# K and Q turned by VectorE in SBUF, chunk bounds and selection by pairs of pairs, fewer multiplied masks, and a new order of work

## The chip, the cores and the metric

The kernel runs on one core of a Trainium2 chip. The core has five engines with an instruction stream each: TensorE (PE; its weight loads are listed apart as PEld), VectorE (DVE), ScalarE (ACT), GpSimd (POOL) and SyncE (SP), which here issues nearly all DMAs. Sixteen DMA engines move the data. The metric is the device time of one execution in microseconds (us).

## The reference

Two layers follow one another. The first is attention on selected chunks: for each query the keys are cut into 24 chunks of 32, an upper bound of the score with any key of a chunk is worked out from the chunk's smallest and largest key, the six best chunks that are not in the future are kept, and softmax runs over them alone. The second is a feed-forward layer with a hard swish.

```python
# q, k, v: (4, 8, 768, 64) fp32; chunk = 32, top_k = 6, scale = 1/8
k_min, k_max = min and max of k over each chunk
ub = sum over d of max(q * k_min, q * k_max)            # (4, 8, 768, 24)
ub = where(query's chunk >= chunk, ub, -1e9)
top_chunks = argsort(ub)[..., -6:]
scores = scale * q @ k.T
scores = where(chunk selected & causal, scores, -1e9)
attn = exp(scores - max) / (sum + 1e-9)
x = (attn @ v) as (3072, 512)
h = x @ w_in                                            # w_in (512, 2048)
out = (h * clip(h + 3, 0, 6) / 6) @ w_out               # w_out (2048, 512)
```

## The kernel before

The 32 heads are worked as 16 pairs, numbered 0 to 15; a pair's two heads e = 0, 1 lie in partitions 0 to 63 and 64 to 127, so that both of a pair's K (or Q) fill 128 partitions with the head dimension along them and the 768 positions along the free axis. Queries below 192 (Q0) see at most six chunks, so nothing is selected for them; the selection is for the other 576.

The whole program is one list of steps, `ORDER` (lines 34 to 111), written out by hand or by a planner that is not part of the file. The loop at line 619 emits the steps in this order, and each engine and the SP queue run what falls to them in it. Semaphores hold an instruction until its inputs are there and its output buffer is free; the order itself is never changed at run time. A late input therefore holds up everything behind it on that engine. A step is named by a short word and its indices, for example `S.7.3.a`: the scores of pair 7, unit 3, into the PSUM buffer a. PSUM holds three large buffers a, b and c (1,024 columns of fp32) and two small ones x and y (512).

For pair i the steps are:

- `lk.i`, `lq.i`, `lv.i`: loads of K, Q and V from DRAM by SP. For K and Q (line 215) there is one DMA for each head, with rows of 64 fp32, 256 bytes, as runs; three buffers each take turns. V is one DMA.
- `K.i`, `Q.i`: six 128x128 fp32 transposes by TensorE (line 298) into a large PSUM buffer, for the load lays positions along the partitions.
- `kb.i`, `qb.i`: ScalarE writes bf16 copies (lines 319 and 329). `mx.i`, `mn.i`: VectorE reduces the chunks of K (line 344). `rp.i`: ScalarE writes the positive part of Q; `rn.i` (VectorE) or `ra.i` (ScalarE) the negative part.
- `U.i`: the bounds, as (positive part of q) times k_max plus (negative part of q) times -k_min, fp32 matmuls into 96 partitions (line 367), and `ub.i`: VectorE adds the causal bias. Or `ud.i`, line 391: the same for the pairs i and i + 1 at once, in 128 partitions, with `us.i` for the bias. Before, pairs 0 to 5 go alone and pairs 6 to 15 in doubles.
- `T.i`: the bounds are transposed by TensorE (lines 403, 408), so that a query's 24 chunks lie along the free axis; `t8.i`: twelve instructions that give the eight largest of 32 (line 413); `sel.i`: each bound against the sixth largest (line 417); `L.i`: TensorE transposes the selection back (line 427); `mt.i`: VectorE copies it to SBUF.
- The mask is used in one of two ways. Pairs with an `sm` step (here 6 to 15) are multiplied: `sm.i` stores the selection to DRAM by four DMAs, `ml.i.j` loads it spread over the 32 keys of each chunk, for key block j, by six DMAs, `am.i.j` (GpSimd) cuts the causal corner, and `mu.i.u` (VectorE, line 463) multiplies the exponentials by it. The other pairs (0 to 5) add a large number to the scores by further matmuls (line 479).
- `S.i.u`: scores of unit u, one of six groups of key and query blocks (line 471); `ex.i.u`: exponentials by ScalarE (line 485); `af.i.u`: causal corner by GpSimd; `A.i`, `B.i.e`: the values (line 508), `na.i`, `nb.i`: normalised by VectorE into the input of the next layer.

The second layer runs over eight groups g of 384 tokens: `xt.g` turns the input by three DMA transposes (groups 0 and 1: `X` by TensorE); `H.g.f` is a pair of 128-wide slices of the hidden layer, eight matmuls (line 552); `hu` (ScalarE) and `gt` (VectorE, line 563) apply the gate; `O.g.t.n` is a quarter of the projection of 128 tokens (line 590), `ot` copies it out on ScalarE and `st` stores it. `wl.n` loads an eighth of the weights in fp32 (0 to 3 of w_in, 4 to 7 of w_out), in two buffers, and `wc.n` casts it to bf16 on GpSimd. These buffers later hold masks.

Of the kernel before, what the change touches and what calls it, by code (L numbers as in the profile page):

```python
# [15 lines left out]
P = 128  # L16
# [3 lines left out]
E_VAL = 8192.0  # L20
# [14 lines left out]
PRD Z.b.12 PRP PRL PRA lk.0 K.0.a lq.0 kb.0 mx.0 mn.0 Q.0.b rp.0 qb.0 lk.1 K.1.c rn.0 U.0.a ub.0 kb.1 mx.1 lq.1  # L35
Q.1.b T.0.x mn.1 t8.0 sel.0 lq.2 Q.2.a lk.2 lv.0 lq.3 lk.3 lv.1 rp.1 qb.1 ra.1 U.1.c ub.1 lk.4 vc.0 lv.2 lq.4
rp.2 qb.2 ra.2 K.2.b kb.2 L.0.y mt.0 S.0.1.c ex.0.1 S.0.2.a T.1.x S.0.3.c ex.0.2 ex.0.3 S.0.5.a ex.0.5 mx.2 mn.2
S.0.0.b ex.0.0 t8.1 sel.1 U.2.c ub.2 S.0.4.a ex.0.4 L.1.y Q.3.b rp.3 mt.1 S.1.1.c ex.1.1 qb.3 T.2.x t8.2 rn.3
K.3.a kb.3 af.0.5 af.0.3 af.0.0 af.0.1 A.0.y S.1.0.c ex.1.0 mx.3 sel.2 mn.3 S.1.4.b ex.1.4 S.1.2.c ex.1.2 L.2.x
S.1.5.b ex.1.5 vc.2 af.0.2 S.1.3.a ex.1.3 U.3.c mt.2 S.2.2.b ex.2.2 S.2.0.a ex.2.0 af.1.0 na.0 af.1.1 ub.3 T.3.x  # L40
t8.3 af.1.3 sel.3 af.2.2 af.1.5 K.4.c lq.5 kb.4 mx.4 S.2.3.b Q.4.a ex.2.3 B.0.0.y L.3.x mt.3 rp.4 lk.5 wl.0 lv.4
lq.7 S.2.1.b ex.2.1 vc.1 wc.0 af.2.0 af.1.2 af.2.1 B.0.1.y qb.4 mn.4 A.1.x S.3.1.b ex.3.1 S.3.2.c ex.3.2 S.2.5.b
ex.2.5 rn.4 U.4.a nb.0 S.3.0.c ex.3.0 na.1 ub.4 S.2.4.b ex.2.4 T.4.y t8.4 sel.4 K.5.a kb.5 mx.5 S.3.5.c ex.3.5
Q.5.b B.1.0.x L.4.y rp.5 mt.4 qb.5 B.1.1.x mn.5 S.4.2.c af.3.0 ex.4.2 rn.5 A.2.y lv.3 S.3.3.a ex.3.3 af.2.5 lk.7
lk.6 lq.8 lq.6 vc.3 wl.2 S.4.1.b U.5.c na.2 nb.1 ub.5 ex.4.1 vc.4 af.3.2 af.2.3 S.4.3.a ex.4.3 af.4.3 af.3.5
af.3.3 bd af.3.1 S.4.4.b ex.4.4 wc.2 af.4.1 af.4.2 T.5.y S.4.0.c S.3.4.a B.2.0.x S.4.5.b ex.4.0 ex.4.5 af.4.0
# [68 lines left out]
def kernel(  # L115
# [115 lines left out]
    def k_turn(i):  # L231
        nc.sync.dma_start_transpose(KB[i % 3][:], SK[i][:])
# [419 lines left out]
```

## Time and profile before

| | |
|---|---|
| median of three timed runs | 282.7 us (282.19 to 283.12) |
| profiled execution | span of 282.4 us, 0.3 us under that median |
| granted clock of TensorE | 1.00 throughout |
| busy: TensorE, VectorE, ScalarE, GpSimd | 271.8, 195.1, 182.1, 72.1 us |
| moved by DMA | 54.39 MB in 107,056 packets |
| of these under 512 B | 86,928 packets |

In the profile a busy time is the union of an engine's instructions. Matmuls are pipelined: one that stands at 379 ns follows the one before it by less, so the prices of TensorE's steps are taken from distances of starts. The page's slices cut the span into 40 equal parts of 7.06 us with the busy share in tenths. The chain of waits is the work that ended last, followed back to what released it. In a row of the groups stand line, engine, operation, output and input with their shapes, the count, the busy sum, the mean of one in ns, and the idle time before it. In a row of the DMA issues stand count, size, and the median time from issue to landing.

### The profile page before, as it was taken

How to read it: one execution, taken by the hardware profiler on the slowest of the kernel's cores; microseconds unless marked ns; L12 is line 12 of the kernel's file. 1: busy time of each engine (PE TensorE's matmuls, PEld its weight loads, DVE VectorE, ACT ScalarE, POOL GpSimd, SP SyncE). 2: the span in 40 equal slices, each digit the busy share in tenths (PEclk: the TensorE clock that was granted, in tenths of full speed). 3: DMA queues.
4: the chain of work that ended last, by engine and by line, in shares of the span. 5: the costliest groups of instructions: out<-in, count | busy, mean ns of one | idle time of the engine just before them, and what ended most of it. 6: DMA issues, size and time to landing. Idle time of an engine off the chain costs nothing.

```text
span 282.4 us, 6943 instructions
## 1 busy us (share of the span) xinstructions
PE 271.8 (96%) x2706; PEld 164.7 (58%) x2706; DVE 195.1 (69%) x523; ACT 182.1 (64%) x242; POOL 72.1 (26%) x138
## 2 busy tenths in 40 slices
PE   8798999899999999998999999999999999999995
PEld 3566777757654666564556566645456646555544
DVE  4787786979898896568975798737935894532330
ACT  2699999988758988452888865753657433433331
POOL 6034294486254031005531120107004100000000
PEclk9999999999999999999999999999999999999999
DMA  8999999979979998599999789998789320111023
GB/s 167 218 201 214 269 218 245 281 230 311 272 227 284 245 195 195 150 273 264 251 278 207 146 183 206 257 294 164 206 255 267 97 40 37 39 56 62 15 75 111
DMA packets 107056, 54.39 MB, mean 193 GB/s; under 512 B 86928, under 2 KB 96144, under 8 KB 107024
## 3 DMA queue, kind: packets, MB, share of 16 engines
q1 hardware_dynamic: 105456, 53.56, 77.8%
q10 hardware_dynamic: 1568, 0.39, 0.7%
q8 instruction: 21, 0.34, 0.6%
q14 instruction: 11, 0.09, 0.1%
HBM read 42.34 MB, written 9.24 MB: 183 GB/s over the span
## 4 chain that ended last, share of the span: by engine, by line
PE 73%; DMA 8%; ACT 5%; SPq 5%; DVE 4%; issue 2%; POOL 1%; ACTq 0%
PE PSy L590 13%; PE PSx L590 11%; PE PBb L552 10%; PE PBa L552 8%; PE PBc L552 8%; ACT PT L485 4%; DMA WS<-in_moe_w_in_dram 3%; PE PSx L508 3%; DMA QS<-in_q_dram 3%; DMA KSM<-in_k_dram 3%; PE PSy L508 2%; PE PBa L298 2%; PE PBc L471 2%; SPq L449 2%; PE PBb L290 2%; PE PBa L471 2%
## 5 line engine op out<-in xcount | busy, mean ns | idle before, releaser
L552 PEld LDWEIGHTS <-WIN 128*128 128x128 bf16 x512 | 48.9, 98 | 32.8 <-issue 1.3
L590 PEld LDWEIGHTS <-GT 128*128 128x128 bf16 x368 | 34.4, 98 | 37.9 <-issue 2.5
L590 PE MATMUL PSy<-WOUT,GT 128*128 128x512 bf16 x208 | 50.5, 379 | 0.0
L590 PE MATMUL PSx<-WOUT,GT 128*128 128x512 bf16 x160 | 38.9, 379 | 0.0
L552 PE MATMUL PBb<-XT,WIN 128*128 128x384 bf16 x192 | 35.1, 326 | 0.0
L485 ACT ACTIVATE PT<-PBc 128x1024 bf16<-128x1024 f32 (+2 forms) x34 | 31.4, 924 | 3.9 <-PE PBc L471 3.2
L485 ACT ACTIVATE PT<-PBb 128x1024 bf16<-128x1024 f32 (+2 forms) x35 | 31.3, 895 | 3.8 <-PE PBb L471 2.0
L456 POOL TENSOR_SCALAR_AFFINE_SELECT WS<-WS 128x256 bf16<-128x256 bf16 x30 | 12.5, 427 | 71.6 <-DMA WS<-SCR 51.8
L560 ACT ACTIVATE U<-PBb 128x768 bf16<-128x768 f32 x24 | 19.5, 811 | 16.3 <-PE PBb L552 16.3
L552 PE MATMUL PBa<-XT,WIN 128*128 128x384 bf16 x160 | 29.3, 326 | 0.0
L563 DVE SCALAR_TENSOR_TENSOR GT<-U,PBb 128x768 bf16<-128x768 bf16 x24 | 22.8, 950 | 9.4 <-ACT U L560 9.1
L552 PE MATMUL PBc<-XT,WIN 128*128 128x384 bf16 x160 | 29.3, 326 | 0.0
L508 PEld LDWEIGHTS <-PT 128*128 128x128 bf16 x672 | 24.8, 98 | 6.1 <-POOL PT L492 1.7
L463 DVE TENSOR_TENSOR PT<-PT,WS 128x256 bf16<-128x256 bf16 (+2 forms) x70 | 27.4, 441 | 0.0
L485 ACT ACTIVATE PT<-PBa 128x1024 bf16<-128x1024 f32 (+2 forms) x27 | 25.8, 954 | 2.0 <-PE PBa L471 1.3
L563 DVE SCALAR_TENSOR_TENSOR GT<-U,PBa 128x768 bf16<-128x768 bf16 x20 | 19.0, 950 | 10.6 <-ACT U L560 10.5
L563 DVE SCALAR_TENSOR_TENSOR GT<-U,PBc 128x768 bf16<-128x768 bf16 x20 | 19.0, 950 | 10.4 <-ACT U L560 10.4
L492 POOL TENSOR_SCALAR_AFFINE_SELECT PT<-PT 128x256 bf16<-128x256 bf16 x56 | 22.2, 420 | 11.6 <-ACT PT L485 11.5
L560 ACT ACTIVATE U<-PBa 128x768 bf16<-128x768 f32 x20 | 16.3, 813 | 13.5 <-PE PBa L552 13.3
L293 POOL CAST VB<-VS 128x768 bf16<-128x768 f32 x16 | 13.5, 850 | 44.5 <-DMA VS<-in_v_dram 44.5
L471 PEld LDWEIGHTS <-KB 64*128 64x128 bf16 x320 | 14.4, 94 | 14.6 <-issue 10.3
L560 ACT ACTIVATE U<-PBc 128x768 bf16<-128x768 f32 x20 | 16.2, 812 | 9.9 <-PE PBc L552 9.6
(125 smaller groups left out, 396.3 us busy)
## 6 DMA issues: line engine op xcount, KB each, us to landing
VS<-in_v_dram SPq DMA_DIRECT2D x16, 384.0 KB, 5.0
KSM<-in_k_dram SPq DMA_DIRECT2D x31, 192.0 KB, 5.0
QS<-in_q_dram SPq DMA_DIRECT2D x31, 192.0 KB, 5.0
out_dram<-OT SPq DMA_DIRECT2D x23, 256.0 KB, 2.3
WS<-in_moe_w_in_dram SPq DMA_DIRECT2D x4, 1024.0 KB, 8.6
WS<-in_moe_w_out_dram SPq DMA_DIRECT2D x4, 1024.0 KB, 6.2
SCR<-MTM SPq DMA_DIRECT2D x40, 72.0 KB, 3.5
WS<-SCR SPq DMA_DIRECT2D x10, 288.0 KB, 5.5
```

Of the source, the lines that this page charges most:

```text
L290: nc.tensor.matmul(PSB[c][:, 0, :], lhsT=WARM[:, 0:P], rhs=WARM, start=True, stop=True)
L293: nc.gpsimd.tensor_copy(VB[i % 4][:, :, :, 0:D], VS[i % 2][:].rearrange("p e j d -> p j e d"))
L456: nc.gpsimd.affine_select(out=T, in_=T, pattern=[[0, 2], [1, P]], compare_op=A.is_ge, fill=0.0, base=0, channel_multiplier=-1)
L463: nc.vector.tensor_tensor(out=T, in0=T, in1=mask_view(i, j, lo, q0 + n), op=A.mult)
L471: nc.tensor.matmul(PSB[c][:, e, at:at + n], lhsT=K[rows, j * P:(j + 1) * P], rhs=Q[rows, q0:q0 + n], start=True, stop=q0 + n <= Q0 or i in ...
L485: nc.scalar.activation(PT[i % 3][u][:, :, 0:n], PSB[slot["S", i, u]][:, :, 0:n], ACT.Exp, scale=float(scale))
L492: nc.gpsimd.affine_select(out=T[:, :, lo:lo + P], in_=T[:, :, lo:lo + P], pattern=[[0, 2], [1, P]], compare_op=A.is_ge, fill=0.0, base=0, ...
L508: nc.tensor.matmul(O[:, e, t, :], lhsT=PT[i % 3][u][:, e, lo:lo + P], rhs=VB[i % 4][:, j, e, :], start=(j == 0), stop=(j == qb))
L552: nc.tensor.matmul(PSB[c][:, ff, 0:GRP], lhsT=WIN[:, kt, (2 * f + ff) * P:(2 * f + ff + 1) * P], rhs=XT[g % 3][:, kt, :], start=(kt == 0), ...
L560: nc.scalar.activation(slot["R", g, f][:], PSB[slot["H", g, f]][:, :, 0:GRP], ACT.Relu, bias=3.0)
L563: nc.vector.scalar_tensor_tensor(out=GT[g % 2][:, 2 * f:2 * f + 2, :], in0=slot["R", g, f][:], scalar=6.0, in1=PSB[slot["H", g, f]][:, :, ...
L590: nc.tensor.matmul(PSS[c][:], lhsT=GT[g % 2][:, f, t * P:(t + 1) * P], rhs=WOUT[:, f, :], start=(f == 0), stop=(f == FT - 1))
```

## The change

**K and Q of pairs 4 to 15** are loaded so that the 32x32 blocks already stand where they belong, but each block is turned: partition group 32d + 64e holds head e's half d of the head dimension, with the position within a chunk along the partitions. Each load is four DMAs, with runs of 32 fp32, 128 bytes. VectorE then turns the blocks in place (`kd.i`, `qd.i`). The K and Q steps on TensorE go away for these pairs; the bf16 copies, reductions and positive parts read SBUF in place of PSUM. Six of the K copies (pairs 5, 7, 9, 11, 13, 15) go from ScalarE to GpSimd (`kp.i`).

**Their bounds** use q itself for the second product: relu(q) times (k_max - k_min) plus q times k_min. So there is no negative part, and a small subtraction (`kx.i`, 24 elements) on VectorE is new.

**Bounds of pairs 2 to 15** go by doubles. `tr.i` turns the 576 columns of bounds by VectorE, `tm.i.e` takes nine maxima each, `se.i` selects for both pairs, and `tb.i` turns the selection back, all in SBUF; T, t8, sel, L and mt are left only for pairs 0 and 1. For pairs 2 to 7 `mr.i` (GpSimd) moves 64 rows of a mask to the partitions where the mask matmuls want them.

**Masks** are multiplied from pair 8 on; pairs 6 and 7 now use the mask matmuls. The selection there is taken as "not selected" and the large number is negative.

**The order** is new throughout. The feed-forward of group 0 starts before the scores of pairs 4 and 5; K, Q, V and the weights are loaded earlier relative to TensorE's work; the activation warm-up `PRA` stands in the middle; nine warm-up matmuls are left of twelve. The negative parts of pairs 0 to 3 now lie in the space of the second layer's output weights, and the buffers of maxima and selections are single. Dead variants of the K and Q loads are removed.

```diff
-E_VAL = 8192.0
+E_VAL = -8192.0
...
 ORDER = """
-PRD Z.b.12 PRP PRL PRA lk.0 K.0.a lq.0 kb.0 mx.0 mn.0 Q.0.b rp.0 qb.0 lk.1 K.1.c rn.0 U.0.a ub.0 kb.1 mx.1 lq.1
...
+lk.1 lk.0 PRD PRP PRL Z.b.9 K.1.b mx.1 K.0.c mn.0 mn.1 kb.0 lq.0 Q.0.a rn.0 kb.1 mx.0 rp.0 lk.2 K.2.b mn.2 U.0.c
...
+hu.0.6 wl.6 wc.6 H.0.3.c hu.0.3 mx.7 mn.7 wl.7 H.1.7.a hu.1.7 O.0.2.0.x wc.7 O.0.0.0.y gt.0.3 rp.7 S.5.2.c ex.5.2
...
+am.12.4 H.4.3.a hu.4.3 am.13.2 ml.13.0 H.4.2.b gt.4.3 hu.4.2 nb.9 H.4.6.c hu.4.6 gt.4.2 qd.14 mu.11.3 ml.13.1
+O.4.1.0.x gt.4.6 S.12.3.a ex.12.3 kd.15 S.11.5.b ex.11.5 O.4.2.0.y O.4.2.1.y O.4.2.2.y O.4.2.3.y mu.11.5 rp.14
+O.4.1.1.x ot.4.2 B.11.0.y kb.14 qd.15 rp.15 mx.15 ml.13.3 am.12.2 B.11.1.y nb.11 xt.5 O.4.1.2.x O.4.1.3.x S.13.0.a
+ex.13.0 af.13.0 S.13.4.b ot.4.1 ex.13.4 mn.15 kx.15 ud.14.c ml.12.3 us.14 tr.14 S.12.4.a mu.12.2 O.3.0.0.y ex.12.4
...
+    KF = [KSM[:, S * n:S * (n + 1)] for n in range(3)]
+    QF = [t[:].rearrange("p j e d -> p (j e d)") for t in QS]
+    TURNK, TURNQ = named("kd"), named("qd")
+    DOUBLE = {x for i in named("ud") for x in (i, i + 1)}
+    PRODUCT = sorted(named("sm"))
...
+    UBT = const.tile([P, 2 * HQ], FP32, name="UBT")
+    SELD = const.tile([P, 2 * HQ // CH, CH], BF16, name="SELD")
+    T8D = const.tile([P, 2 * HQ // CH, 8], FP32, name="T8D")
...
+    RN = [WOUT[:, 3 * n:3 * n + 3, :].rearrange("p a b -> p (a b)").bitcast(FP32)[:, 0:NQ] for n in range(2)]
...
+    def load_turned(dst, x, i):
+        b, hp = divmod(i, NPAIR)
+        for e in range(2):
+            for d in range(2):
+                g = D * e + CH * d
+                nc.sync.dma_start(dst[g:g + CH].rearrange("p (n d) -> p n d", d=CH),
+                                  x[b, 2 * hp + e].rearrange("(n t) d -> t n d", t=CH)[:, :, CH * d:CH * (d + 1)])
...
+    def turn_k(i):
+        nc.vector.transpose(out=KF[i % 3], in_=KF[i % 3])
+
+    def turn_q(i):
+        nc.vector.transpose(out=QF[i % 3], in_=QF[i % 3])
...
+    def k_bf16_pool(i):
+        nc.gpsimd.tensor_copy(KB[i % 3][:], k_turned(i))
...
+    def k_span(i):
+        T = KM[i % 3][:, :, 0:NCH]
+        nc.vector.tensor_tensor(out=T[:, 0], in0=T[:, 0], in1=T[:, 1], op=A.subtract)
...
+    def q_parts(i):
+        return RP[i % 2][:], q_turned(i, Q0) if i in TURNQ else RN[i % 2]
...
+    def turn_double(i):
+        nc.vector.transpose(out=UBT[:], in_=UBD.rearrange("p e n -> p (e n)"))
+
+    def top8_double(i, e):
+        view = UBT[:].rearrange("p (s c) -> p s c", c=CH)
+        for s in range(9 * e, 9 * e + 9):
+            nc.vector.max(out=T8D[:, s, :], in_=view[:, s, :])
+
+    def select_double(i):
+        nc.vector.tensor_tensor(out=SELD[:], in0=UBT[:].rearrange("p (s c) -> p s c", c=CH),
+                                in1=T8D[:, :, TOPK - 1:TOPK].to_broadcast([P, 2 * HQ // CH, CH]),
+                                op=A.is_ge if i in PRODUCT else A.is_lt)
+
+    def turn_back(i):
+        nc.vector.transpose(out=MTD[(i // 2) % 2].rearrange("p e n -> p (e n)"), in_=SELD[:].rearrange("p s c -> p (s c)"))
+
+    def move_rows(i):
+        e, T = 1 - i % 2, MTD[(i // 2) % 2]
+        g = 64 * (i % 2)
+        nc.gpsimd.tensor_copy(MS[i % 2][64 * e:64 * e + 64], T[g:g + 64, e])
```

## The prediction

> **What bounds the kernel now.** I read the page's shares and slices first, then the busy time by stage, then the chain of waits, then the groups for prices. A step is named as in the order list (ud.14: double bounds of pairs 14 and 15).
>
> The page: TensorE is busy 96% of the span, and the DMA engines stand at 8 or 9 tenths in most slices until slice 31, then are nearly idle.
>
> ```profile
> PE 271.8 (96%) x2706; PEld 164.7 (58%) x2706; DVE 195.1 (69%) x523; ACT 182.1 (64%) x242; POOL 72.1 (26%) x138
> ...
> DVE  4787786979898896568975798737935894532330
> ...
> PEclk9999999999999999999999999999999999999999
> DMA  8999999979979998599999789998789320111023
> ```
>
> By stage (columns: stretch, its length, busy time of PE, weight load, DVE, ACT, POOL, then clock, DMA share, GB/s): PE loses 6.6 us in the first 70 us and 1 us in the next 148. The DMA share is 0.93 to 1.03 up to 219 us, so the transfers are close behind. The last two rows give rates: the first holds only loads in runs of 256 B, the other mostly masks.
>
> ```profile
> 0.00:70.60 70.60, 64.02 (x955) 44.80 (x956) 54.22 (x185) 59.36 (x78) 34.84 (x68) 1.00 1.03 235
> 70.60:141.20 70.60, 69.80 (x621) 40.54 (x619) 57.02 (x142) 48.27 (x65) 19.66 (x32) 1.00 0.94 236
> 141.20:218.90 77.70, 77.55 (x737) 45.31 (x737) 54.73 (x150) 52.01 (x69) 16.34 (x36) 1.00 0.93 224
> 218.90:282.40 63.50, 60.47 (x400) 34.01 (x397) 29.14 (x47) 22.46 (x33) 1.24 (x3) 1.00 0.19 59
> ...
> 7.10:14.10 7.00, 5.01 (x67) 3.48 (x68) 5.22 (x12) 4.81 (x8) 0.00 (x0) 1.00 1.35 218
> 183.60:190.60 7.00, 7.00 (x67) 3.30 (x66) 2.58 (x3) 3.58 (x6) 0.13 (x1) 1.00 1.02 293
> ```
>
> The chain of waits is TensorE almost alone from 57 us. It also prices TensorE's steps: six fp32 turns 0.66 us, a double bounds 1.13.
>
> ```profile
> 183.26 0.66 PE PBa L298 x6
> ...
> 186.94 1.13 PE PBa L391 x32
> 188.07 1.41 PE PBb L552 x8
> ...
> 191.20 0.33 PE PSy L403 x3
> ```
>
> Groups and DMA issues, for the prices of VectorE (951 ns to read 768 fp32 a lane, 758 for 576) and of the loads:
>
> ```profile
> L344 DVE TENSOR_REDUCE KM<-PBa 128x24 f32<-128x768 f32 x20 | 18.4, 951 | 3.0 <-ACT KB L319 3.0
> L396 DVE TENSOR_TENSOR UBM<-PBa,BIASM 128x576 f32<-128x576 f32 x3 | 2.3, 758 | 2.6 <-PE PBa L391 2.6
> ...
> KSM<-in_k_dram SPq DMA_DIRECT2D x31, 192.0 KB, 5.0
> SCR<-MTM SPq DMA_DIRECT2D x40, 72.0 KB, 3.5
> ```
>
> The profiled execution spans 282.4 us; the runs' median is 282.7, so a sum against the span stands 0.3 under the runs.
>
> **TensorE, part by part** (distance of one matmul's start from the next in the trace, as they are pipelined). Removed: 144 fp32 turns of K and Q at 109 ns, 15.7; 30 turns of double bounds at 0.33 to 0.37 per three, 3.7; 16 of single ones, 1.6; 42 turns of selections, 2.4; four single bounds at 0.85, 3.4; three warm-up matmuls, 1.3. Added: two double bounds, 2.3; the mask matmuls of pairs 6 and 7, 28 a pair, 1.65 us a pair, 3.3. Net 22.5 less. If nothing else moved: 282.4 - 22.5 = 259.9.
>
> **VectorE.** Removed: maxima of 14 pairs at 1.2 us, 16.8; their selections at 0.55, 7.7; mask copies at 0.30, 4.2; mask products of two pairs, 7.6 (37.8 busy for ten pairs); four bias adds, 2.2; five negative parts, 3.7: 42.2. Added: 24 turns of 128x768 fp32. No such instruction is in the trace: below, 0.59 us (the product of 128x768 bf16); above, 1.9 (twice the reduction). I take the reduction's 0.95, the same input read once: 22.8. Then seven turns of 576 fp32, seven selections, seven turns back and two bias adds at 0.76, 17.5; 126 maxima at 0.10, 12.6; twelve spans of 24 elements, 0.2 each, 2.4. In all 55.3, net 13 more: 195 becomes 208, 179 of it in a stretch of about 209 us where 166 of 219 was. No bound, but less slack.
>
> **ScalarE, GpSimd, start.** ScalarE loses seven negative parts (0.67) and six K casts (0.80), 9.5 us, hidden beside TensorE. GpSimd gains those casts at 0.85 and six row moves (nearest: a 0.42 us select), 7.6, plus as many selects of scores as it loses of masks: 80 of 282, hidden; uncovered it costs the 7.6. The activation warm-up goes to mid-order: 0 to 1.3 us at the start.
>
> **Transfers: the price of the gain.** Each turned load becomes four DMAs with 3,072 runs of 128 B for 1,536 of 256. SP issues 257 DMAs for 229: 48 more loads, 8 fewer mask stores, 12 fewer mask loads. A 256 B run costs an engine 16 x 256 B / 218 GB/s = 18.8 ns; no 128 B run is in the trace. Below: half, 9.4 (bytes alone count); above: 18.8 (runs alone count). The packet records give medians of 9 ns for the 4 B semaphore writes, 18 for 256 B, 29 for 576, 84 for 2048: a straight line with a fixed part of 9, on which 128 B cost 13.3 to 14.1. I take 14: 3,072 x 14 / 16 = 2.7 us a load for 1.8; 24 loads, +21 (0 to +43). Masks of two pairs fall away: 2 x (1.47 MB at 293 GB/s = 5.1, and stores 0.9) = 12. So transfers grow by 9 us while TensorE's work shrinks by 22.
>
> One rule speaks against the change. The Trainium skill, "DMA: Bandwidth & Descriptors", section "How a descriptor splits into AXI transactions", says a read must begin at a 256 B boundary, and the bytes before its start still cost beats: the half rows at offset 128 would cost a whole run. By that the mean would be (14 + 18.8) / 2 = 16.4 ns and my sum 283, no gain; no run shown here starts off a boundary, so the trace can't say.
>
> **Where transfers and TensorE meet.** The last K and Q load is now Q of pair 14, issued after 8 loads of 256 B, 24 turned ones, 14 of V, 8 weights, 5 mask stores, 27 mask loads, 3 x transposes and 10 stores. By DMA time, in that order: 8 x 1.8 = 14.4, 24 x 2.69 = 64.6, 14 x 1.8 = 25.2, 8 x 2.7 (512 packets at 84 ns) = 21.6, 5 x 0.93 = 4.7, 27 x 0.86 = 23.1, 3 x 1.73 (1,536 packets at 18 ns) = 5.2, 10 x 0.67 = 6.7: 165.5. Where SP's issue time is longer (four stores 2.8 us, three transposes 3.8) it is 181.0. Add 0.8 for the start and 4.9 to landing: 171 or 187. The same sums for the last K load before (32 loads, 13 of V, 8, 6, 36, 3 and 6 of the others) are 154 and 171; it landed near 175, 4 past the upper, with TensorE waiting for none of it. So the landing lies between 171 and 191; I take the middle, 181.
>
> The turn now waits on VectorE: behind qd.14 stand mu.11.3 and gt.4.6, and O.4.2.3 needs gt.4.6: 0.95 + 0.6 + 0.95 = 2.5. Behind O.4.2.3 TensorE has 48 O at 0.865, 24 H at 1.30, 22 score groups 4.9, 14 value groups 6.3, one double bounds 1.1: 85.1. Before, the same prices give 92.2 from ud.14 on, and the trace took 282.4 - 186.9 = 95.5: factor 1.035, so 88.1. Sum: 181 + 2.5 + 88.1 = **272**; 262 and 282 for the two landings.
>
> An early check: O.0.2.2 needs the seventh weight load, behind 14.4, nine turned loads 24.2, four of V 7.2 and, with its own, seven weights 18.9: 64.7, + 5.7, cast 1.9: 72.3. TensorE has 186.3 behind it, x 1.035 = 192.8: 265. So the weights alone, moved ahead of the PE work that covered them, return 5 of the 22.5.
>
> **The rivals.**
> 1. *128 B runs cost nearly what 256 B ones do* (ends slower). Each ns moves the landing by 24 x 192 = 4.6 us; from 272 the sum passes 282.7 at 16.3 ns. At 18.8 it is 294, at 17 it is 286. For it: the first stretch's 218 GB/s against 293 for long runs, so runs count. Against: the fixed part is 9 of 18.
> 2. *VectorE becomes the bound*: a turn at 1.9, and its 14 smaller kin at 1.5, add 33: 212 of 209 us, so some 10 us over the forecast with its waits, 282 to 286. It passes no change from about 1.8 us a turn. Against: the reduction reads the same at 0.95. "VectorE: DVE Perf Modes" of the skill, section "The three transpose paths", has 311 ns for a 128x128 bf16; six give 1.9 by its figure, an estimate that no row here can test.
> 3. *The transfers hide*: TensorE alone, 260 to 264. For it: DMA gaps before were partly lack of demand. Against: the DMA share of 0.93 to 1.03.
>
> **How the numbers follow.** The forecast (264 to 281) 0.47; rival 1 0.28; rival 2 0.10; rival 3 0.12; an order that loses as much as it saves 0.03. A measurement of this kernel tells about 0.3% from no change. Faster: 0.47 + 0.12 + 0.02 of rivals 1 and 2 = 0.61; slower 0.26 + 0.08 + 0.01 = 0.35; same 0.04. The time is the likeliest case's, 272. The range is 260, TensorE's own sum, to 292, which leaves out rival 1 from 18.4 ns up, under 2 in 10.
>
> **What would show it.** Right: turned loads near 2.7 us a pair when loads run alone (145 GB/s); PE busy near 249 with 15 to 25 us idle, most of it before 75 us and behind gated waits on turns; VectorE's turn near 0.95; DMA share near 1 up to 215 us. Wrong: under 130 GB/s in those stretches (rival 1), VectorE at 95% in the middle with turns over 1.6 us (rival 2), PE idle under 12 us (rival 3).

## The result, and the profile after

The changed kernel took 293.92 us (median of three runs, 291.25 to 297.70), against 282.7 before: a ratio of 1.036, 95% interval 1.029 to 1.044, so slower. The ratio leaves out the run of 297.70 us, which fell into a slower state that some executions show. Forecast were 272 us, with a range of 260 to 292. A second set of runs gave 293.42 and 1.042 (1.037 to 1.047). The profiled execution took 291.25 us with a span of 289.5.

The page of the changed kernel, its shares, three rows of slices, the packets and the chain by engine:

```profile
PE 254.2 (88%) x2473; PEld 146.2 (50%) x2495; DVE 208.0 (72%) x483; ACT 175.1 (60%) x229; POOL 79.9 (28%) x150
...
PE   6296869989979999798896999997799999999995
...
PEclk9859999999999999999999899999999999999999
DMA  8929999989989989889999999786997683020103
...
DMA packets 141807, 50.76 MB, mean 175 GB/s; under 512 B 124240, under 2 KB 131664, under 8 KB 141776
...
PE 39%; DMA 19%; SPq 18%; DVE 9%; issue 6%; POOL 5%; ACT 2%; DVEq 0%; POOLq 0%; ACTq 0%
```

TensorE was busy 271.8 us before and is now busy 254.2; the work did shrink. But it is idle for 35.3 us where it was idle for 10.6. Its share of the chain of waits fell to 39%, and DMA and SP's queue hold 37% of it. New is a granted clock below full speed in two places.

By stage (columns as before: PE, weight load, DVE, ACT, POOL, then clock, DMA share, GB/s):

```profile
0.00:70.60 70.60, 54.62 (x681) 35.99 (x682) 57.01 (x149) 45.03 (x58) 31.14 (x57) 0.93 0.95 203
70.60:141.20 70.60, 62.57 (x659) 34.86 (x667) 53.83 (x127) 46.44 (x62) 21.52 (x38) 1.00 0.93 197
141.20:218.90 77.70, 70.73 (x611) 38.12 (x617) 62.06 (x145) 49.32 (x64) 18.84 (x38) 0.98 0.95 206
218.90:289.50 70.60, 66.25 (x525) 37.21 (x530) 35.11 (x65) 34.34 (x47) 8.45 (x18) 1.00 0.33 92
```

TensorE now loses 16 us in the first 70 us, 8 in the second, 7 in the third and 4 in the last (6.6, 0.8, 0.2 and 3 before). The DMA share is as high as it was. So the loss isn't at one place, and the transfers are as full as before.

The new operations, in the groups of VectorE, and the turned loads, in the DMA issues (the last number is the median time from issue to landing):

```profile
L236 DVE STREAM_TRANSPOSE QS<-QS 128x768 f32<-128x768 f32 x12 | 11.6, 970 | 5.4 <-DMA QS<-in_q_dram 5.4
L233 DVE STREAM_TRANSPOSE KSM<-KSM 128x768 f32<-128x768 f32 x12 | 11.6, 966 | 4.9 <-DMA KSM<-in_k_dram 4.9
L400 DVE TENSOR_TENSOR SELD<-UBT,T8D 128x576 bf16<-128x576 f32 x7 | 6.0, 853 | 0.1
L392 DVE STREAM_TRANSPOSE UBT<-UBM 128x576 f32<-128x576 f32 x7 | 5.4, 775 | 0.2
```

```profile
KSM<-in_k_dram SPq DMA_DIRECT2D x48, 96.0 KB, 4.0
QS<-in_q_dram SPq DMA_DIRECT2D x48, 96.0 KB, 3.2
```

A turn costs 0.97 us (forecast 0.95), a turn of 576 columns 0.775 (0.76). The packet records give 13.3 ns for a run of 128 B, mean over 73,728 (forecast 14). The prices were right; the time was not.

### The profile page after: what moved, and what is told of

The parts are those of the page before. It is cut to its first block, busy times and chain, and to the rows that moved or that the text cites. A ratio compares the mean times of both kernels' runs of the same rounds, so it can differ in the third digit from the quotient of the medians.

```text
span 289.5 us, 6516 instructions
## 1 busy us (share of the span) xinstructions
PE 254.2 (88%) x2473; PEld 146.2 (50%) x2495; DVE 208.0 (72%) x483; ACT 175.1 (60%) x229; POOL 79.9 (28%) x150
## 4 chain that ended last, share of the span: by engine, by line
PE 39%; DMA 19%; SPq 18%; DVE 9%; issue 6%; POOL 5%; ACT 2%; DVEq 0%; POOLq 0%; ACTq 0%
SPq L217 10%; PE PSy L591 8%; PE PSx L591 7%; PE PBa L553 5%; PE PBb L553 5%; DMA VS<-in_v_dram 5%; PE PBc L553 4%; DMA QS<-in_q_dram 4%; DMA KSM<-in_k_dram 3%; SPq L450 3%; SPq L535 3%; DMA WS<-in_moe_w_in_dram 2%; DVE KM L326 2%; DMA WS<-in_moe_w_out_dram 2%; SPq L445 2%
## 5 line engine op out<-in xcount | busy, mean ns | idle before, releaser
L493 POOL TENSOR_SCALAR_AFFINE_SELECT PT<-PT 128x256 bf16<-128x256 bf16 x64 | 25.6, 422 | 46.7 <-ACT PT L486 41.1
L486 ACT ACTIVATE PT<-PBa 128x1024 bf16<-128x1024 f32 (+2 forms) x33 | 30.9, 935 | 9.7 <-PE PBa L472 7.0
L553 PE MATMUL PBa<-XT,WIN 128*128 128x384 bf16 x184 | 33.7, 326 | 1.2 <-ACT PT L486 0.7
L553 PE MATMUL PBb<-XT,WIN 128*128 128x384 bf16 x152 | 28.2, 329 | 7.3 <-DMA XT<-XB 3.7
L553 PE MATMUL PBc<-XT,WIN 128*128 128x384 bf16 x176 | 32.2, 326 | 0.3 <-POOL WIN L249 0.3
L564 DVE SCALAR_TENSOR_TENSOR GT<-U,PBa 128x768 bf16<-128x768 bf16 x23 | 21.8, 947 | 12.9 <-ACT U L561 12.6
L486 ACT ACTIVATE PT<-PBc 128x1024 bf16<-128x1024 f32 (+2 forms) x29 | 27.6, 953 | 4.6 <-PE PBc L480 2.6
L561 ACT ACTIVATE U<-PBa 128x768 bf16<-128x768 f32 x23 | 18.7, 811 | 13.5 <-PE PBa L553 13.3
L464 DVE TENSOR_TENSOR PT<-PT,WS 128x768 bf16<-128x768 bf16 (+2 forms) x56 | 22.9, 447 | 4.3 <-ACT PT L486 2.4
L561 ACT ACTIVATE U<-PBb 128x768 bf16<-128x768 f32 x19 | 15.4, 811 | 16.9 <-PE PBb L553 16.9
L561 ACT ACTIVATE U<-PBc 128x768 bf16<-128x768 f32 x22 | 17.8, 811 | 12.4 <-PE PBc L553 12.4
L564 DVE SCALAR_TENSOR_TENSOR GT<-U,PBb 128x768 bf16<-128x768 bf16 x19 | 18.0, 946 | 6.3 <-ACT U L561 6.1
L326 DVE TENSOR_REDUCE KM<-KSM 128x24 f32<-128x768 f32 x24 | 22.1, 936 | 0.1
```

The lines of the kernel that those rows point to most:

```text
L326: nc.vector.tensor_reduce(out=KM[i % 3][:, m, 0:NCH], in_=k_turned(i).rearrange("p (c w) -> p c w", w=CH), axis=AX.X, op=(A.max, A.min)[m] ...
L464: nc.vector.tensor_tensor(out=T, in0=T, in1=mask_view(i, j, lo, q0 + n), op=A.mult)
L486: nc.scalar.activation(PT[i % 3][u][:, :, 0:n], PSB[slot["S", i, u]][:, :, 0:n], ACT.Exp, scale=float(scale))
L493: nc.gpsimd.affine_select(out=T[:, :, lo:lo + P], in_=T[:, :, lo:lo + P], pattern=[[0, 2], [1, P]], compare_op=A.is_ge, fill=0.0, base=0, ...
L553: nc.tensor.matmul(PSB[c][:, ff, 0:GRP], lhsT=WIN[:, kt, (2 * f + ff) * P:(2 * f + ff + 1) * P], rhs=XT[g % 3][:, kt, :], start=(kt == 0), ...
L561: nc.scalar.activation(slot["R", g, f][:], PSB[slot["H", g, f]][:, :, 0:GRP], ACT.Relu, bias=3.0)
```

## The experiments

"Behind its work" below is, as in the expectations, the start of a step of TensorE less the summed prices of all its steps before it. All ratios are to the kernel before, run on the same chip beside each. Line numbers move by up to eight with an edit.

| kernel | median us | ratio, 95% interval |
|---|---|---|
| changed kernel, second time (h0) | 293.42 | 1.042, 1.037 to 1.047 |
| Q of pair 0 early (e1) | 288.23 | 1.022, 1.017 to 1.027 |
| twenty warm-up matmuls (e2) | 289.03 | 1.025, 1.019 to 1.030 |
| runs of 256 B, two DMAs (e3) | 277.68 | 0.984, 0.980 to 0.989 |
| runs of 256 B, four DMAs (f1) | 283.55 | 1.006, 1.004 to 1.008 |
| K, Q loads cut to 16 KB (g1) | 274.76 | 0.973, 0.969 to 0.977 |
| the same, and Q of pair 0 early (g2) | 270.96 | 0.959, 0.954 to 0.964 |
| V loads cut (h2) | 284.89 | 1.008, 1.005 to 1.011 |
| first half twice (h3) | 294.14 | 1.042, 1.037 to 1.047 |
| half the turned DMAs on ScalarE (f2) | 299.59 | 1.060, 1.056 to 1.063 |
| that, Q of pair 0 early, stores on ScalarE (f3) | 299.53 | 1.059, 1.052 to 1.066 |
| no K, Q turns on VectorE (g4) | 293.23 | 1.038, 1.033 to 1.043 |
| Q of pair 14 early (h1) | 296.14 | 1.051, 1.047 to 1.055 |
| order before, K and Q of 4 to 15 turned (e4) | 311.15 | 1.100, 1.094 to 1.106 |
| order before, K and Q of 12 to 15 turned (g3) | 288.58 | 1.024, 1.018 to 1.030 |
| order before, selection of 6 to 15 by VectorE (e5) | 283.02 | 1.005, 1.002 to 1.008 |
| e1, masks of 8 and 9 by matmul (h4) | 279.14 | 0.990, 0.985 to 0.995 |
| e1, masks of 8 to 11 by matmul (h5) | 283.12 | 1.002, 0.999 to 1.006 |

Starts of some steps of TensorE in us, from the traces; these kernels share one order of its steps:

| | changed | e1 | e3 | f1 | g1 | g2 | h2 |
|---|---|---|---|---|---|---|---|
| Q.0 | 13.4 | 9.2 | 13.3 | 14.8 | 13.2 | 9.2 | 13.3 |
| Q.3 | 27.5 | 22.7 | 27.6 | 27.2 | 27.5 | 22.6 | 26.3 |
| ud.4 | 41.8 | 36.5 | 41.6 | 41.6 | 41.4 | 36.6 | 41.5 |
| ud.8 | 91.3 | 87.4 | 87.1 | 87.8 | 88.0 | 81.8 | 91.0 |
| ud.12 | 153.6 | 152.7 | 147.1 | 147.6 | 147.5 | 139.2 | 148.1 |
| O.4.2.3 | 197.1 | 194.9 | 186.7 | 187.2 | 184.8 | 176.3 | 189.2 |
| H.6.3 | 241.8 | 239.1 | 229.6 | 234.1 | 228.0 | 220.0 | 233.4 |

### The start: one DMA behind a copy on ScalarE

The load of Q of pair 0 is two DMAs, and line 210 puts the second on ScalarE's queue. Before, `lq.0` stood ahead of `kb.0`, and that DMA was issued at 1.43 us. In the new order `lq.0` stands behind `kb.0`. ScalarE in time order, changed kernel (start, duration, engine, line; in brackets the idle time ahead and what ended it):

```profile
8.93 0.80 ACT L313 CAST KB<-PBc 128x768 bf16<-128x768 f32 x1 [6.32 <-DVE KM L326]
8.94 0.37 ACTq L210 DMA_DIRECT2D QS<-in_q_dram  x1
```

The copy waits for two reductions on VectorE, and the DMA waits behind the copy. The chain of waits of the same kernel carries it to TensorE:

```profile
7.05 1.86 DVE KM L326 x2
8.94 4.32 DMA QS<-in_q_dram
13.39 1.53 PE PBa L291 x6
```

Q.0 starts at 13.4 us where it started at 7.2 before, and its six turns take 1.53 us, where the six of K.1, at 6.2 us in the same kernel, took 0.86. SP then sits until the turns of Q.2 free a buffer: its queue is still from 14.0 to 19.7 us, and the DMA row of slices shows a 2 there.

```diff
-lk.1 lk.0 PRD ... kb.0 lq.0 Q.0.a
+lk.1 lk.0 lq.0 PRD ... kb.0 Q.0.a
```

> The changed kernel with one step moved: lq.0 directly behind lk.0, so that the half of Q of pair 0 that ScalarE's queue issues no longer stands behind kb.0. Theory A (the start: that DMA, issued at 8.9 us, holds Q.0 to 13.4 us, and the pause lowers TensorE's clock): Q.0 starts before 9.5 us, the turns behind it take 0.66 to 0.84 us and not 1.53, TensorE lies about 8 to 10 us behind its own work at 42 us in place of 20, and the time is 281 to 287. Theory C (transfers set the pace from 80 us on, whatever the start does): TensorE gains at the start and gives it back by 125 us; 290 to 294.

Measured: 288.23 us, between the two theories' figures. Q.0 starts at 9.2 us. Its own turns still take 1.49 us, against theory A, for in this execution TensorE ran at half rate until 10.7 us; those of K.2 behind them take 0.88. TensorE lies 14.4 us behind its work at ud.4, not 19.6; I had expected 8 to 10. Against the second set of runs of the changed kernel that is 5 us less, 1.9% of the time before. Part of the lead shrinks on the way (5.2 us at ud.4, 2.7 at H.6.3 in the profiled executions). So theory A holds for the place and falls short in size.

The other way round, the wait kept and TensorE kept busy:

```diff
-... kb.0 lq.0 Q.0.a
+... kb.0 lq.0 Z.a.20 Q.0.a
```

> The changed kernel with twenty more warm-up matmuls of 0.43 us in front of Q.0, where TensorE waits anyway; Q of pair 0 lands as late as before. It parts the clock from the wait. If the low clock is most of the loss at the start: the turns behind Q.0 take 0.66 us each instead of 1.53, and the time falls by 4 to 6 us, to 287 to 290. If the wait alone counts: less than 1.5 us. If the warm-up itself is in the way: Q.0 later than 13.9 us and the time unchanged or longer.

Measured: 289.03 us, 4.4 under the changed kernel, with Q.0 as late as before (13.2 us). TensorE in time order, first the changed kernel, then the one with warm-ups:

```profile
13.39 1.51 PE L291 MATMUL PBa<-IDENT,QS 128*128 128x128 f32 x6 [5.49 <-DMA QS<-in_q_dram]
14.70 1.49 PE L291 MATMUL PBb<-IDENT,KSM 128*128 128x128 f32 x6
```

```profile
13.20 0.85 PE L291 MATMUL PBa<-IDENT,QS 128*128 128x128 f32 x6 [1.30 <-DMA QS<-in_q_dram]
13.88 0.82 PE L291 MATMUL PBb<-IDENT,KSM 128*128 128x128 f32 x6
```

The turns of K and Q run at twice the rate, Q.2 is reached at 17.8 us in place of 20.1, and SP's next load goes out at 17.6 in place of 19.7. So at the start keeping the clock up is worth nearly what taking the wait away is. Both act at the same place; together they were not tried.

### Transfers: how long a run, how many issues, how many bytes

```diff
-            load_turned(KF[i % 3], k, i)
+            load(KS[i % 3], k, i)
...
-            load_turned(QF[i % 3], q, i)
+            load(QS[i % 3], q, i)
```

> The changed kernel with the K and Q loads of pairs 4 to 15 in runs of 256 B, two DMAs each instead of four (as for pairs 0 to 3); VectorE turns as before, so the K and Q of these pairs are not in the right layout, and the output is not the reference's; the work of every engine is the same. Transfers shrink by 24 x 0.9 = 21 us and SP issues 48 DMAs less. Theory C (the turned loads set the pace): 268 to 277, the start as slow as in the changed kernel. Theory A (the start alone): 288 to 294.

Measured: 277.68 us, 16 under the changed kernel with all engines' work kept. The start is as slow as there; the lead comes from ud.4 on. That is about theory C's figure, but not by its arithmetic. From the packet records, the summed time of all packets on the sixteen engines, divided by sixteen, is 217.9 us here and 229.4 in the changed kernel (second profile): 11.5 us less, not 21, for under load a run of 256 B takes 22.4 ns and two of 128 B take 26.6. SP's issues take 164.4 us and not 207.7. To part the two:

```diff
+    def load_split(dst, x, i):
+        b, hp = divmod(i, NPAIR)
+        for e in range(2):
+            for n in range(2):
+                nc.sync.dma_start(dst[:, 3 * n:3 * n + 3, e, :],
+                                  x[b, 2 * hp + e, 384 * n:384 * n + 384].rearrange("(j p) d -> p j d", p=P))
```

> The kernel with runs of 256 B once more (K and Q of pairs 4 to 15 not in the right layout, so the output is not the reference's), but each of their loads in four DMAs of 384 runs in place of two of 768: as many issues on SP as in the changed kernel (257), and the packets of the 277.7 us kernel. Theory D (SP's issuing is the scarce thing: SP spends 207.7 us on its DMAs in the changed kernel, 164.4 with two DMAs a load): the time goes back most of the way, to 285 to 291, and the issue of one such DMA stays above 0.5 us. Theory C (the packets' time on the DMA engines): 276 to 280.

Measured: 283.55 us, between the two theories' figures. Four issues a load for two cost 6 us, and the other 10 go with the runs of 128 B. These 10 are not parted further: beside this kernel the changed one has 12.6 us more of packets (229.4 for 216.8), and SP spends 33 us more on its issues (207.7 for 174.9). So SP's time may hold a share of them; no run tried it by itself. For the 6 us theory D's mechanism isn't seen: one issue of a K or Q load took 0.49 us (median; 0.5 to 0.7 in the changed kernel), and at O.4.2.3 this kernel is only 0.6 us behind the one with two DMAs. The rest comes later, in the wait for the second layer's input, which three DMA transposes turn. Waits of TensorE between 186 and 240 us, with four DMAs:

```profile
PE PBb L552 <- DMA XT<-XB: 2.2, 2, 2.1
```

Chain of waits, with four DMAs, then with two:

```profile
193.96 5.22 DMA XT<-XB
199.31 1.60 PE PBb L552 x8
200.91 2.56 PE PBa L552 x8
```

```profile
192.98 3.73 DMA XT<-XB
196.85 1.46 PE PBb L545 x8
198.31 1.30 PE PBa L545 x8
```

The landing is 1.5 us later, TensorE waits 2.1 us, and then eight matmuls take 2.56 us instead of 1.30: a clock drop behind a short wait. Why that landing is later was not settled.

With nearly no transfer for these loads:

```diff
     def load_turned(dst, x, i):
         b, hp = divmod(i, NPAIR)
-        ... four DMAs
+        nc.sync.dma_start(dst[0:CH, 0:4 * CH].rearrange("p (n d) -> p n d", d=CH),
+                          x[b, 2 * hp].rearrange("(n t) d -> t n d", t=CH)[:, 0:4, 0:CH])
```

> The changed kernel with each K and Q load of pairs 4 to 15 cut to one DMA of 128 runs of 128 B (16 KB of 393 KB; the rest of the tile keeps older values, so the output is not the reference's). Every engine's work is the same; the transfers lose 24 x 2.5 = 60 us of the DMA engines' time and SP issues 72 DMAs less. If transfers and SP's queue are all that holds TensorE back after the start: TensorE stays near the 20 us that it has lost by 42 us, and the time is 266 to 271. If VectorE's chains (turn, reduce, bounds, turn, maxima) or the order hold it too: 273 to 280.

Measured: 274.76 us, and 270.96 with `lq.0` early:

> The kernel before this one with lq.0 directly behind lk.0 as well. If the start's loss stands by itself and nothing refills it: 4 to 6 us under the 16 KB kernel without it. If that loss is covered by something later: under 2 us. What remains above 260 (TensorE's own sum) is what neither transfers nor the late Q of pair 0 explain.

The page of the second of these, with its packets:

```profile
PE 249.8 (93%) x2473; PEld 144.6 (54%) x2495; DVE 205.7 (77%) x483; ACT 174.8 (65%) x229; POOL 80.3 (30%) x150
...
DMA packets 69998, 41.70 MB, mean 156 GB/s; under 512 B 52432, under 2 KB 59856, under 8 KB 69968
```

The first kernel is above its 266 to 271 and inside the other forecast, 273 to 280, by which VectorE's chains or the order hold TensorE too. It is only 3 us under the 256 B version, though its packets take 55 us less (162.8). So the first 11.5 us of the turned loads' packets, with 48 issues, are worth 16 us, and the next 55 only 3. The start gives 4 us more, as it did with whole loads. What is left over 260, some 11 us, is neither: in the second kernel TensorE lies 14.4 us behind its work at ud.4 and 19.4 at H.6.3, and where it waits in the first 42 us it waits 1.8 us for a copy of K behind the reductions and 3.0 us for VectorE's first selections.

Whether it must be K and Q:

```diff
+        if i >= 4:
+            nc.sync.dma_start(VS[i % 2][0:CH, 0, 0, :], v[b, 2 * hp, 0:CH, :])
+            return
```

> The changed kernel with each V load of pairs 4 to 15 cut to 32 runs of 256 B (the rest keeps older values; the output is not the reference's); the K and Q loads are whole. Takes 12 x 1536 x 21.9 ns / 16 = 25 us off the DMA engines. If any transfer's time is worth the same (60 us less of K and Q gave 18): 6 to 10 us less, 282 to 287. If it is the turned loads themselves, with their many runs: within 3 us of the changed kernel.

Measured: 284.89 us, 8.5 under the changed kernel run beside it, for packets that take 28.5 us less (200.9). So loads that were not changed at all count too, 0.3 us for each us of packets, as the cut of K and Q in all (19 for 67): it is the transfers in sum that hold TensorE back, not the turned loads alone. Why the step from 128 B to 256 B is worth more than its packets was not settled.

The rule that the prediction weighed (the Trainium skill, "DMA: Bandwidth & Descriptors", section "How a descriptor splits into AXI transactions"), tried by itself:

```diff
-... [:, :, CH * d:CH * (d + 1)])
+... [:, :, 0:CH])
```

> The changed kernel with every turned DMA reading the first 32 columns of its rows, so that all runs of 128 B begin at a multiple of 256 B (both halves of the head dimension get the first half; the output is not the reference's). If runs that begin 128 B further cost more, as a page of the Trainium skill has it (DMA: Bandwidth & Descriptors, How a descriptor splits into AXI transactions): the mean of a 128 B packet falls from 13.3 to about 10 ns or lower, and the time by 4 us or more. If not: 13.0 to 13.6 ns and no change beyond 1.5 us.

Measured: 294.14 us, with 13.3 ns for the mean packet of 128 B (in a profiled execution of 298.13 us), as in the changed kernel. A run that starts 128 B into a block of 256 cost nothing extra here.

### SP's queue relieved

```diff
-                nc.sync.dma_start(dst[g:g + CH]...
+                queue = nc.scalar if e == 1 else nc.sync
+                queue.dma_start(dst[g:g + CH]...
```

> The changed kernel with the two turned DMAs of head 1 of each K and Q load issued by ScalarE's queue, the other two by SP: 128 B packets as before, 48 issues fewer on SP and 48 more on ScalarE (at about 0.57 us each 27 us, ScalarE then busy or issuing for 202 us). Theory D: 276 to 284. Theory C: within 2 us of the changed kernel, 289 to 294. A third outcome, slower than 295: ScalarE's stream, held up by its own DMA issues, becomes late for the exponentials.

> Three changes to the changed kernel at once, a try at the best version: lq.0 directly behind lk.0, the turned DMAs of head 1 on ScalarE's queue, and the 23 output stores on ScalarE's queue behind the copies that they wait for (SP waited 27 us for those copies). Theory A gives 4 us (as measured for the first alone), theory D another 8 to 15 for the second and third: 270 to 279. Theory C: 284 to 289.

Measured: 299.59 and 299.53 us, the third outcome, though not by the cost of the issues (50 of them took 20.5 us in all, 0.32 us for most). ScalarE issues a load in its own order, and the exponentials wait behind it. In the longest such wait it was not the buffer that was missing: its last readers, the turns of K.3 on TensorE, had ended by 33 us. The two DMAs of K of pair 6 that ScalarE issues go out at 37.50 and 44.70 us, the second one 0.02 us after the landing of a V load that counts on the same semaphore. ScalarE in time order, its wait, then TensorE's waits between 30 and 52 us, in the first of the two kernels:

```profile
37.50 7.51 ACTq L218 DMA_DIRECT2D KSM<-in_k_dram  x2
```

```profile
ACT PT L487 <- DMA KSM<-in_k_dram: 8.2, 1, 8.2
```

```profile
PE PBb L473 <- ACT PT L487: 7.7, 2, 7.4
```

That the stores and the early Q gave nothing on top shows only that this loss covers them; the stores alone were not tried.

### VectorE's turns left out

```diff
-"kd": turn_k, "qd": turn_q,
+"kd": lambda i: None, "qd": lambda i: None,
```

> The changed kernel without the 24 turns of K and Q on VectorE; the loads stay as they are, and what read the turned tile reads the loaded one (the output is not the reference's). VectorE loses 24 x 0.95 = 23 us, and its stream no longer waits for a load at a turn, but at the reduction behind it. If VectorE's own time holds TensorE back: 6 us or more below the changed kernel, 280 to 286. If transfers do: 288 to 292.

Measured: 293.23 us, a ratio of 1.038 against 1.042: no gain, with 19 us less on VectorE:

```profile
PE 254.9 (87%) x2473; PEld 146.4 (50%) x2495; DVE 189.3 (65%) x459; ACT 174.6 (60%) x229; POOL 81.3 (28%) x150
```

### The landing that was to set the end

In the changed kernel Q of pair 14 lands at 194.6 us, and VectorE waits for it (VectorE in time order):

```profile
191.30 0.94 DVE L564 SCALAR_TENSOR_TENSOR GT<-U,PBb 128x768 bf16<-128x768 bf16 x1
194.57 0.98 DVE L236 STREAM_TRANSPOSE QS<-QS 128x768 f32<-128x768 f32 x1 [2.33 <-DMA QS<-in_q_dram]
...
196.11 0.95 DVE L564 SCALAR_TENSOR_TENSOR GT<-U,PBc 128x768 bf16<-128x768 bf16 x1
```

O.4.2.3 starts at 197.1, 2.5 us after the landing, just as the prediction had it. The base and the kernel with that load moved ahead:

> The changed kernel itself, as the base of the three beside it: 290 to 294.

```diff
-... lk.14 nb.8 ...   (lk.15 and lq.14 some 40 and 70 steps later)
+... lk.14 lq.14 lk.15 nb.8 ...
```

> The changed kernel with lq.14 and lk.15 directly behind lk.14, some 35 us earlier in SP's list; the loads of masks and V and the stores between go later by the time of two loads. The prediction had the end set by the landing of Q of pair 14, at O.4.2.3. If that one landing sets it: TensorE reaches O.4.2.3 some 6 to 10 us earlier, and the time falls to 282 to 287. If the transfers as a whole pace TensorE, step by step: TensorE lies 36 us behind its work just before that place and 38 behind it, so at most 2 us are to be had, and what is put off costs as much: 289 to 295.

Measured: 296.14 us beside 293.42. The load is issued by 175 us, and VectorE reaches its turn only at 199.0, with no wait. TensorE now waits elsewhere, for a transposed input whose DMAs stand behind the two loads on SP. VectorE's row, and TensorE's longest wait between 140 and 215 us:

```profile
199.03 0.97 DVE L237 STREAM_TRANSPOSE QS<-QS 128x768 f32<-128x768 f32 x1
```

```profile
PE PBa L554 <- DMA XT<-XB: 6.4, 1, 6.4
```

That landing does not set the end. It was merely the next thing late in a queue where all was late.

### Parts of the change in the order before

K and Q alone:

```diff
-K.4.c ... Q.4.a ... rn.4 U.4.a     (and so on for pairs 4 to 15)
+kd.4 ... qd.4 ... kx.4 U.4.a
```

> The kernel before, in its own order, with only K and Q of pairs 4 to 15 loaded turned and turned by VectorE (kd and qd where K and Q stood, kx behind the second reduction, no negative part; lq.7, lq.8 and lk.9 stand up to 19 steps later, for they must follow the last reader of the buffer). TensorE loses 15.7 us of turns; transfers grow by 21 us. Theory C: the transfers, which filled 0.93 to 1.03 of the first 219 us before, push the end out: 288 to 298. Theory A together with the new order as the cause of the loss: 268 to 276. Between: both.

Measured: 311.15 us, far beyond theory C's 288 to 298. The page's rows:

```profile
PE   8797669569759983999979799959999999999996
...
PEclk9999697967989998799999999997999999999999
```

The old order puts the turn where TensorE's turns stood, close behind the load and close ahead of its use, so, as I read it, TensorE waits from 30 us on; it runs at half clock for 34 us of the span. The place of the turn was not tried by itself. The changed kernel, with its new order and the other parts, is 18 us below this. With four pairs only:

> The kernel before, in its own order, with only K and Q of pairs 12 to 15 loaded turned and turned by VectorE. TensorE loses 48 turns of 109 ns, 5.2 us; transfers grow by 8 loads of 0.4 to 0.9 us, 3 to 7 us, and VectorE by 8 turns less four negative parts and four small steps, some 6 us. If the loss of the twelve-pair version (29 us) lies in the early stretch, where TensorE has little work per byte: 277 to 281. If it is spread evenly over the pairs: 29 x 4 / 12 = 10 more, 290 to 294.

Measured: 288.58 us, 6.8 over the kernel before and between the two forecasts. Here TensorE's longest wait is behind VectorE, which gets to a gate late, behind the chain of a late K (load, turn, two reductions):

```profile
PE PSy L581 <- DVE GT L554: 4.2, 1, 4.2
```

The selection alone:

```diff
-T.7.x t8.7 ... T.6.y sel.7 t8.6 sel.6 ... L.6.x L.7.y mt.6 mt.7
+tr.6 tm.6.1 ... tm.6.0 se.6 tb.6
```

> The kernel before, in its own order, with only the selection of the doubles 6 to 15 by VectorE in SBUF (tr, tm, se, tb where T, t8, sel and L, mt stood for the first time of the pair, tm and se at the second). TensorE loses 20 turns of the bounds of 0.33 to 0.37 us per three and 10 of selections, about 3.7 + 1.5 = 5 us; VectorE gains ten turns of 0.77 and loses ten copies and half of the maxima and selections. If the sum by TensorE's steps holds: 277 to 279. If VectorE's two turns stand in the way (mask late, TensorE or the mask stores wait): 282 to 286.

Measured: 283.02 us, 1.005, inside the second forecast. TensorE's work fell (268.2 us busy for 271.8), and the time did not. But in the profiled execution (286.33 us) its longest wait is 2.6 us for a Q load, not one for VectorE's turns, so the reason given with that forecast isn't shown.

### Trading transfers for matmuls

```diff
-sm.8 ml.8.3 ml.8.1 ... am.8.3 ... mu.8.1 ...   (all of pairs 8 and 9)
+mr.8 mr.9 (behind tb.8), af.8.2 af.8.3 af.8.5 af.9.2 af.9.3 af.9.5
-    MS = ring(2, [P, HQ], BF16, "MS")
+    MS = ring(4, [P, HQ], BF16, "MS")
```

> A try at a version faster than both: the changed kernel with lq.0 directly behind lk.0, and with the masks of pairs 8 and 9 added by matmuls, not multiplied (their stores, loads, cuts and products go, 28 mask matmuls a pair, the row moves on GpSimd and the causal cuts of three more units come; four buffers for the moved rows). TensorE gains 3.3 us of work, the DMA engines lose about 10 us, VectorE 7.6. If transfers pace TensorE at 0.3 to 1 us for each of their own: 281 to 288. If TensorE's added work counts in full and the transfers' relief does not: 290 to 292.

Measured: 279.14 us, 0.990 (0.985 to 0.995): 1% under the kernel before, and below the forecast of 281 to 288. Its packets take 208.7 us, 19.7 less than with `lq.0` moved alone (228.4); 12 of it are the masks' own packets, the rest comes off the mean of the others (256 B: 20.8 ns for 22.0). By stage between 105 and 175 us, the changed kernel (second profile), then this one:

```profile
105.00:140.00 35.00, 31.81 (x333) 18.10 (x332) 24.19 (x55) 21.92 (x30) 7.99 (x17) 0.95 0.93 200
140.00:175.00 35.00, 32.28 (x292) 16.76 (x292) 30.57 (x70) 25.19 (x33) 12.43 (x25) 1.00 0.94 216
```

```profile
105.00:140.00 35.00, 34.41 (x341) 19.39 (x342) 25.01 (x54) 25.77 (x36) 7.32 (x15) 1.00 0.60 120
140.00:175.00 35.00, 33.30 (x346) 19.12 (x347) 26.38 (x65) 23.71 (x30) 9.53 (x20) 1.00 0.91 211
```

The DMA share falls to 0.60 in the first of these stretches, and TensorE is busy for 3.6 us more over both, the added matmuls included. Beside the kernel with `lq.0` moved alone, ud.12 starts at 145.8 us in place of 152.7. VectorE has 10 us less to do too (200.0 us busy for 210.2); as 19 us less of its work gave nothing (g4), I put the gain down to the transfers, but no run parted the two. Two more pairs:

> The same for pairs 8 to 11: TensorE gains 6.6 us, the DMA engines lose about 20, VectorE 15. If transfers pace TensorE: 278 to 285, below the kernel with two such pairs. If not: 292 to 295, above it.

Measured: 283.12 us, within 278 to 285 but above the first. Up to O.4.1.0 TensorE is 0.8 us behind it with the added matmuls in hand, and then comes a new wait, for a causal cut on GpSimd (TensorE's waits between 175 and 210 us), with 6.8 us at half clock:

```profile
PE PSy L506 <- POOL PT L490: 3.6, 1, 3.6
```

The cut stands in GpSimd's order behind the mask cuts of another pair, for whose loads GpSimd idles 9.1 us. So the trade gains with two pairs and is spent with four.

## Why the prediction was wrong

**TensorE's account: right.** 22.5 us less were forecast, and the page has 17.6 less busy (22 of the 2,495 matmuls have no record). Of the 254.2, 11.1 were spent at half clock, so half of that, 5.6, is time that full clock would have saved; it leaves 248.6 against "near 249". The idle time is 35.3 us where 15 to 25 were the sign of being right. Rival 3's figure, 260, is this sum, and no kernel with whole loads came near it.

**VectorE: right.** 208.0 us busy, where 208 was forecast; turn, maxima and kin within 0.12 us each, and without the turns (g4) nothing is gained. Rival 2 is out.

**The price of a run of 128 B: right; the growth of transfers: nearly.** 13.3 ns for 14, and 5.5 us more of packets (229.4 in the second profile for 223.9) for 9. Rival 1 as written is out, and the extra cost of half the runs, which the prediction weighed beside it, was not seen (h3). But its outcome came, 286 to 294, by another way.

**The step that failed is "Where transfers and TensorE meet".** The landing of Q of pair 14 was put at 171 to 191, with 181 taken; it came at 194.6. Behind it the 2.5 us held, and the 88.1 behind O.4.2.3 were 92.4; 194.6 + 2.5 + 92.4 = 289.5, the span. The lower sum, 165.5 of DMA time and 5.7 about it, can be set against the packet records up to 194.6 us, which hold 183.0:

| | forecast us | measured us |
|---|---|---|
| turned loads | 64.6 | 61.4 |
| other runs of 256 B (plain loads, V, transposes) | 44.8 | 52.5 |
| runs of 2048 B (weights, stores) | 28.3 | 34.2 |
| masks and what is left | 27.8 | 31.7 |
| 4 B semaphore writes | 0 | 3.2 |
| engines idle, start and end | 5.7 | 11.6 |

The uncertain price was bounded with care, and the known ones were read wrongly: medians (18 and 84 ns) or the rate of a quiet stretch, where a sum needs means. The records of before give 21.3 ns for 256 B and 96.1 for 2048 B. With these two, the 38,400 and 5,376 packets of the sum give 51.1 and 32.3 us, and it comes to 181.5 and not 171, before any more idle time.

**The second fault is that one meeting point stood for all.** Moving that load (h1) gains nothing. TensorE was already 36 us behind its work at O.4.1.0, before it: 20 of it by 42 us, 5 more by 115, 11 more by 190. The upper sum by SP's time had the same fault: it added durations and no waits, and SP's queue alone stood still for 5.7 us at the start.

**The start: missed.** "0 to 1.3 us" was read from the activation warm-up alone. `lq.0` had moved behind `kb.0`, and one of its two DMAs is ScalarE's. Moving it back is worth 5 us. All in all TensorE has lost 13 us more at 42 us than before; the other 8 belong to the first pairs' chains and were not taken apart.

**The early check** said 72.3 us for O.0.2.2; it came at 80.4, and the same term failed. The way to it was right: TensorE waited 0.9 us there for the cast of the seventh load of weights. But that load landed at 78.4 us, not at 70.4; SP had come to issue it only at 72.4. GpSimd, then TensorE in time order:

```profile
78.44 1.89 POOL L249 CAST WOUT<-WS 128x2048 bf16<-128x2048 f32 x1 [4.12 <-DMA WS<-in_moe_w_out_dram]
```

```profile
80.39 1.02 PE L591 MATMUL PSx<-WOUT,GT 128*128 128x512 bf16 x4 [0.88 <-POOL WOUT L249]
```

**Not foreseen at all: the clock.** It was 1.00 throughout before, so no term stood for it.

What stays open: the 11 us between the kernel with small loads and early Q, and 260; why runs of 128 B cost more of the end than of the DMA engines, and how much of that is SP's issuing; and why four issues a load delay a transposed input by 1.5 us.

## What to carry to other kernels

When work is moved off the bound engine, the cover for transfers goes with it: sum the transfers up to each stage with the mean price under load, taken from the records, not the median, and compare every stage with the shrunken work, not the last landing alone. Look for each DMA of a moved step on the queue that issues it, and at what that queue's engine waits for ahead of it. And where transfers set the pace, trading a piece of them for matmuls can pay: here two pairs' masks, 3.3 us of matmuls for 12 of packets, turned a loss of 2% into a gain of 1%.

## What the hardware showed

**The granted clock.** In the twenty profiles the clock halves for 3.41 us or a multiple of it, 53 times within the work. Each time TensorE had been busy for 0.53 or less of the 3.41 us before; after none of some 1,470 windows that stayed at full clock had it been busy for less than 0.40 of the one before. Between 0.40 and 0.53 it went both ways. A wait of 2.5 us was enough (155.1 us in the changed kernel). The Trainium skill, "TensorE: Matmul & The Clock Gate", section "Part 1: The HAM clock gate", has the same window of 3.4 us, but an idle one as the condition; here half a window of idling did it. So a wait of about two microseconds can cost more than itself: up to 1.7 us for each window at half clock, half its length, an estimate from the 3.41 us. Of the 53 drops, 41 lasted one window, and 12 lasted two to four.

**The first full clock can come late.** The clock's records begin between 4.2 and 26.8 us into the span, and the rows print 1.00 for the time before, though TensorE runs at half rate there. In the changed kernel they begin at 4.9 us in the first profile, where the six turns of K.1 took 0.85 us, and at 26.8 us in the second, where they took 1.51.

**Runs of 128 B from DRAM into SBUF** took 13.1 to 13.7 ns on a DMA engine in every kernel that had them, wherever in a block of 256 B they began, beside 20.8 to 23.7 for 256 B in the same kernels.

**What a packet costs does not follow the sum of packets alone.** With 19.7 us fewer of them (h4 against e1) the mean of an unchanged 256 B packet fell from 22.0 to 20.8 ns; with 63.6 us fewer (g2 against e1) it stayed at 22.0.
